# Attention and gated layer on one core: nine rows of q and k to a partition for pairs 1 to 4, and a new order at the start

## The chip, the core and the metric

The kernel runs on one core of a Trainium2 chip. The core has TensorE (PE) for matrix products, VectorE (DVE), ScalarE (ACT) and GpSimd (POOL) for everything else, and 16 DMA engines that move data between the chip's memory and the on-chip buffers. Matrix products are written to the PSUM buffer, all other tiles lie in SBUF, with 128 partitions each. DMAs are issued by SyncE (SP), ACT or POOL. The metric is the time of one execution on the device in microseconds; the median of three runs is given.

## What is computed

Eight batches of eight heads attend over 576 positions of width 64. To the scores a decay is added that depends on the running sum of a second input `s`; then comes a causal softmax. The heads' outputs, side by side, are 4608 rows of 512, and go through two layers with a gated activation between them.

```python
def _attn_ref(q, k, v, s):
    scale = 1.0 / np.sqrt(D)
    scores = scale * np.matmul(q, k.transpose(0, 1, 3, 2))
    causal = np.triu(np.ones((S, S), dtype=bool), k=1)
    cum = np.cumsum(np.maximum(s, 0.0), axis=-1)
    bias = -(cum[:, :, :, None] - cum[:, :, None, :])
    scores = np.where(causal, -1000000000.0, scores + np.minimum(bias, 0.0))
    attn = np.exp(scores - np.max(scores, axis=-1, keepdims=True))
    attn = attn / (np.sum(attn, axis=-1, keepdims=True) + 1e-09)
    return np.matmul(attn, v)

def _moe_ref(x, w_in, w_out):
    h = x @ w_in                      # x: 4608 x 512, w_in: 512 x 2048
    g = h * np.clip(h + 3.0, 0.0, 6.0) / 6.0
    return g @ w_out
```

## The kernel before

Two heads form a pair; a pair has 2 x 576 = 1152 rows of q and as many of k, nine blocks of 128 (`NTR`). There are 32 pairs, and four of them make a batch.

Each row of q and k is widened from 64 to 68 columns (`XW`): three more columns of k hold the running sum, split into three half-precision parts (hi, mid, lo), against ones in q, and one more column of q holds the negated sum against a one in k. A matrix product of the widened rows is then the score with its decay. For the scores both must lie with these 68 columns along the partitions, so PE transposes each block of 128 rows, and a copy brings the result from PSUM to `qkT`, which has three slots (`NS`); rows 64 to 127 of a slot also serve a mask that later pairs use.

The first four pairs (`FIRST`) and pair 4 take their sums from columns, in the tile `x0`, which lies in memory that the layers need later. `load_part` (line 203) reads q or k of a pair so that a partition gets one row of each block, 256 bytes a piece. `first_columns` (line 746) makes the running sums for five pairs at once: DVE scans 90 rows of 64 values of `s`, PE multiplies with a constant `sums` that is loaded from memory, which turns the sums into columns and adds what stands before each row, and DVE and ACT write the parts. `cast_first` (773) casts q or k into `x0`, `turn_first` (776) transposes and copies. `scores_half` (397) forms one half of a head's causal scores in two PSUM banks, the mask added by a product of the identity with a triangle `tri`, and one exponential on ACT writes them to `Pm`. `attend` (426) multiplies with v; a column of ones gives the divisor; `x_transpose` (461) puts the result into `xT`, the input of the layers.

The order of the work is written out by hand: instructions run on each engine in the order of the program, with no scheduler. At the start a few products of zeros (`keep_warm`, 586) run on PE. Then a loop over eight heads (lines 822 to 859) gives, per head: first half of the scores, a transposition of the next pair, second half, and the head before through `attend`. POOL casts rows and values in between and issues the loads of `w_in`.

After these eight heads the first block of 512 rows goes through the first layer (`m1`, split into `m1_sum` and `m1_act`), while `decay_scan` and `decay_rows` compute sums for all heads, `store_aug` sends those of pairs 5 to 9 out to be read back as rows, and `decay_columns` and `decay_order` bring the others into the tile `dec`, for pairs from 10 on, which are transposed by DMA. Then pair 4 is cast and transposed (lines 889 to 897), and `second_pair` (648) handles pairs 4 to 8, with parts of the second layer (`m2`) between. There the scores go one bank at a time through `scores_bank` (338), and POOL sets the masked elements to zero after each exponential. From pair 9 on `weave` mixes attention and layers by weights. `copy_columns` (247) fills the mask columns of the tile that the DMA transposes; `mask_rows` (190) copies mask rows to the slots.

Of the kernel before, what the change touches and what calls it, by code (L numbers as in the profile page):

```python
# [16 lines left out]
def kernel(  # L17
# [25 lines left out]
    PW = 1664  # L43
# [22 lines left out]
    def pair_of_banks(b):  # L66
# [4 lines left out]
    NG = COLS * W2 // 64  # L71
    g = np.arange(NG)
    sel_np = g[:, None] == g[None, :]
    low_np = (g[:, None] < g[None, :]) & (g[:, None] // 9 == g[None, :] // 9)
    sums_dram = nc.inline_tensor(
        np.ascontiguousarray(
            np.stack([m[:, k::2] for k in range(2) for m in (sel_np, low_np)], axis=1)
        ).astype(np.float32),
        name="sums",
    )  # L80
# [28 lines left out]
    dec = cpool.tile([128, NTR, 4, NP], F16, tag="c_dec")  # L109
# [13 lines left out]
        "p (a t i c) -> p a t i c", a=COLS, t=NTR, i=2  # L123
    )

    s_first = work.tile([NG, 64], F32, tag="s_first", bufs=1)
    sums = work.tile([NG, 4, NG // 2], F32, tag="sums", bufs=1)
    scan = work.tile([NG, 64], F32, tag="scan", bufs=1)
    rest = work.tile([128, NG // 2], F32, tag="rest", bufs=1)
# [29 lines left out]
    def mask_view(sl, i):  # L159
# [4 lines left out]
    nc.vector.memset(x0[:, :, :, 0, D:D + 3], 1.0)  # L164
    nc.vector.memset(x0[:, :, :, 1, D + 3:D + 4], 1.0)
    both = [[0, 2], [1, SEQ]]
    select(
        mask_view(0, 1), both, 4 * GRAN, -GRAN, -16384.0,
        warm[64:128, 0:1].unsqueeze(1).to_broadcast([64, 2, SEQ]),
    )  # L170
    select(ident, [[1, 128]], 0, -1, 0.0, one[:, 0:1].to_broadcast([128, 128]))
    select(ident, [[-1, 128]], 0, 1, 0.0)

    def key_rows():
        nc.vector.memset(one[:, 1:2], 1.0)
        k_rows = mask_view(0, 0)
        select(
            k_rows, both, 4 * GRAN, -GRAN, 0.0,
            one[64:128, 1:2].unsqueeze(1).to_broadcast([64, 2, SEQ]),
        )  # L180
        select(k_rows, [[0, 2], [-1, SEQ]], -4 * GRAN + GRAN - 1, GRAN, 0.0)
        select(tri, [[1, 128]], 0, -1, -65504.0, warm[:, 0:128])
# [6 lines left out]

    def mask_rows(sl, i):  # L190
        nc.vector.tensor_copy(out=mask_view(sl, i), in_=mask_view(0, i))
# [8 lines left out]
    def qk_tile(p):  # L200
        qk_f[p] = work.tile([128, NTR, 2, D], F32, tag="qkf", bufs=3, name=f"qkf{p}")

    def load_part(p, i, t0, t1, eng):
        b, h0 = (2 * p) // H, (2 * p) % H
        rows = (q, k)[i][b, h0:h0 + 2].rearrange("h s d -> (h s) d")
        eng.dma_start(  # L206
            out=qk_f[p][:, t0:t1, i, :],
            in_=rows.rearrange("(t p) d -> p t d", p=128)[:, t0:t1, :],
        )
# [27 lines left out]
    def cast_qk(p):  # L237
        t = work.tile([128, NTR, 2, D], F16, tag="qkh", bufs=2)
        nc.gpsimd.tensor_copy(out=t, in_=qk_f.pop(p))
        qk_h[p] = t  # L240
# [32 lines left out]
    def decay_order():  # L273
        dv = dec_f.rearrange("p i (t a h) -> p t i a h", t=NTR, h=2)
        for r0, r1, j0, j1, h in (
            (0, 128, 0, 4, 0), (0, 64, 4, 5, 0), (64, 128, 4, 5, 1), (0, 128, 5, 9, 1)
        ):
            for i in range(3):
                nc.gpsimd.tensor_copy(
                    out=dec[r0:r1, j0:j1, i, :], in_=dv[r0:r1, j0:j1, i, :, h]  # L280
                )
        nc.gpsimd.tensor_scalar_mul(out=dec[:, :, 3, :], in0=dec[:, :, 0, :], scalar1=-1.0)

    def cast_columns(p):
        x = xb[:, p % 2]
        nc.gpsimd.tensor_copy(  # L286
            out=x.rearrange("p (i t) c -> p t i c", i=2)[:, :, :, 0:D], in_=qk_f.pop(p)
        )
        nc.gpsimd.tensor_copy(out=x[:, NTR:2 * NTR, D:D + 3], in_=dec[:, :, 0:3, p])
        nc.gpsimd.tensor_copy(out=x[:, 0:NTR, D + 3:D + 4], in_=dec[:, :, 3:4, p])  # L290
# [105 lines left out]

    def scores_half(hd, half):
        p, hh = hd // 2, hd % 2
        sl = p % NS
# [4 lines left out]
        for kt, lo, hi, c in parts:  # L404
            ops.append((
                c, hi - lo, kT[:, sl, off + 128 * kt:off + 128 * (kt + 1)],
                qT[:, sl, off + lo:off + hi],
# [18 lines left out]
    def attend(hd, qts=range(5)):  # L426
# [5 lines left out]
        block = BLOCK0 if p < FIRST else BLOCK  # L432
# [28 lines left out]
    def x_transpose(p):  # L461
# [10 lines left out]
        pX = f16(PS[:, 4 if p + 1 < FIRST else 2, :], 640) if p < FIRST else f16(bank("S"), 640)  # L472
# [130 lines left out]
    def scores(hd):  # L603
        return [(lambda bi=bi: scores_bank(hd, bi), 400) for bi in range(4)]
# [43 lines left out]
    def second_pair(p, fill):  # L648
# [27 lines left out]
        if first:  # L676
            transpose_group(p + 1, 0)
        if p + 3 < PTD:
# [67 lines left out]
    def first_columns():  # L746
# [6 lines left out]
        key_rows()  # L753
        cT = PS[:, 7, 0:NG // 2]
        for half in range(2):
            o = cT[64 * half:64 * half + 64, :]
            nc.tensor.matmul(
                out=o, lhsT=scan, rhs=sums[:, 2 * half, :], start=True, stop=False
            )
            nc.tensor.matmul(  # L760
                out=o, lhsT=scan[:, 63:64].to_broadcast([NG, 64]), rhs=sums[:, 2 * half + 1, :],
                start=False, stop=True,
            )
        c3 = cT.rearrange("p (a t) -> p a t", a=COLS)
        r3 = rest.rearrange("p (a t) -> p a t", a=COLS)
        hi, mid, lo = (x0[:, :, :, 1, D + j] for j in range(3))
        nc.vector.tensor_copy(out=hi, in_=c3)
        nc.scalar.activation(out=x0[:, :, :, 0, D + 3], in_=hi, func=AF.Copy, scale=-1.0)
        nc.vector.tensor_tensor(out=r3, in0=c3, in1=hi, op=ALU.subtract)
        nc.vector.tensor_copy(out=mid, in_=r3)  # L770
        nc.vector.tensor_tensor(out=lo, in0=r3, in1=mid, op=ALU.subtract)
# [172 lines left out]
```

The softmax here doesn't subtract the row's maximum and nothing guards it: scores larger than these inputs give would overflow.

## Time and profile before

| | us |
|---|---|
| median of three runs (359.52 to 360.73) | 360.02 |
| profiled execution | 359.87 |
| its span | 358.2 |

| engine or part | what the profile has |
|---|---|
| ACT busy | 208.8 us (58%) |
| DVE busy | 182.9 us (51%) |
| POOL busy | 153.3 us (43%) |
| granted PE clock, mean | 0.999 |

The span is the time from the first instruction to the last one's end; what lies around it is 1.7 us in this execution. Busy time of PE is modelled, as products overlap, so a busy PE isn't necessarily one at its peak. How busy each engine is in the stages:

```profile
0.00:12.00 12.00, 9.75 (x70) 5.28 (x71) 5.69 (x18) 5.50 (x8) 8.97 (x20) 1.00 0.96 197
12.00:20.00 8.00, 7.94 (x143) 6.80 (x141) 5.85 (x11) 6.16 (x9) 5.25 (x7) 1.00 0.89 182
20.00:30.00 10.00, 9.54 (x128) 6.72 (x126) 6.24 (x11) 5.43 (x8) 6.42 (x10) 1.00 1.18 208
30.00:45.00 15.00, 15.00 (x91) 7.66 (x90) 12.44 (x22) 9.94 (x16) 7.49 (x17) 1.00 1.06 215
45.00:60.00 15.00, 14.04 (x162) 9.24 (x161) 8.09 (x18) 8.26 (x19) 10.80 (x26) 1.00 1.02 220
```

The columns are the stretch and its length, busy time and number of instructions of PE, of PE's weight loads, DVE, ACT and POOL, the granted clock, the mean busy share of the DMA engines, and the gigabytes per second that they moved.

### The profile page before, as it was taken

The numbers are of one execution on the slowest core, as the hardware profiler recorded it, in microseconds if no ns is written. First come the engines' busy times: TensorE is split into PE (matmuls) and PEld (weight loads), VectorE is DVE, ScalarE is ACT, GpSimd is POOL, SyncE is SP. The second block draws the span as 40 slices with busy tenths as digits, with TensorE's granted clock in tenths as the row PEclk, the third lists the DMA queues.
The fourth block names the chain that finished last, engine by engine and source line by source line (L and its number), as shares of the span: only waits on it lengthen the run. The fifth ranks groups of instructions, "written<-read, shape, count | busy, mean of one in ns | idle before, by whom it ended". The sixth has DMA issues, their size and how long they took to land.

```text
span 358.2 us, 7700 instructions
## 1 busy us (share of the span) xinstructions
PE 349.6 (98%) x2860; PEld 204.2 (57%) x2860; DVE 182.9 (51%) x314; ACT 208.8 (58%) x391; POOL 153.3 (43%) x378
## 2 busy tenths in 40 slices
PE   7999999999999999999999999999999999999996
PEld 3875557665655555555555555555555544544444
DVE  3758737766534553455435553545255536544531
ACT  3777437668847774677467755776477614533410
POOL 6694377765654444444444554555543200000000
PEclk9999999999999999999999999999999999999999
DMA  8999999999989999999998999999947110000012
GB/s 180 214 193 214 212 228 223 215 208 203 210 180 229 197 197 221 229 210 185 185 249 172 207 204 211 170 208 211 224 87 116 50 59 30 31 30 29 32 59 88
DMA packets 185312, 59.09 MB, mean 165 GB/s; under 512 B 177576, under 2 KB 180050, under 8 KB 185274
## 3 DMA queue, kind: packets, MB, share of 16 engines
q1 hardware_dynamic: 181681, 54.05, 72.0%
q0 software_dynamic: 2688, 4.19, 6.6%
q8 instruction: 22, 0.36, 0.4%
q10 hardware_dynamic: 905, 0.36, 0.4%
q14 instruction: 16, 0.13, 0.1%
HBM read 37.32 MB, written 9.53 MB: 131 GB/s over the span
## 4 chain that ended last, share of the span: by engine, by line
PE 84%; DVE 4%; ACT 3%; DMA 3%; POOL 3%; issue 1%; SPq 1%; POOLq 0%; ACTq 0%; DVEq 0%
PE PS L506 32%; PE PS L549 32%; PE PS L348 10%; PE PS L436 7%; DMA qkf<-in_k_dram 3%; DVE gT L517 2%; ACT trl L516 2%; DVE qkT L319 1%; ACT Pm L356 1%; PE PS L569 1%; PE PS L474 1%; PE PS L304 1%; POOL gT L774 1%; PE PS L414 1%; SPq L206 1%
## 5 line engine op out<-in xcount | busy, mean ns | idle before, releaser
L517 DVE SCALAR_TENSOR_TENSOR gT<-trl,PS 128x512 f16<-128x512 f32 x144 | 98.2, 687 | 103.0 <-ACT trl L516 102.9
L516 ACT ACTIVATE trl<-PS,bias 128x512 f32<-128x512 f32 x144 | 98.8, 692 | 78.3 <-PE PS L506 76.5
L506 PE MATMUL PS<-xT,w_in 128*128 128x512 f16 x576 | 143.2, 380 | 0.8 <-DVE gT L517 0.7
L549 PE MATMUL PS<-w_out_sb,gT 128*128 128x512 f16 x560 | 138.9, 379 | 0.0
L356 ACT ACTIVATE Pm<-PS 128x384 f16<-128x384 f32 x224 | 103.0, 507 | 45.7 <-PE PS L348 44.5
L361 POOL TENSOR_SCALAR_AFFINE_SELECT Pm<-Pm 128x256 f16<-128x256 f16 x224 | 68.4, 307 | 114.1 <-ACT Pm L356 106.3
L506 PEld LDWEIGHTS <-w_in 128*128 128x128 f16 x576 | 61.4, 114 | 45.7 <-issue 2.0
L549 PEld LDWEIGHTS <-gT 128*128 128x128 f16 x560 | 51.4, 98 | 48.2 <-issue 0.3
L348 PE MATMUL PS<-qkT 128*128 128x256 f16 x392 | 63.4, 261 | 0.8 <-DVE qkT L319 0.2
L348 PEld LDWEIGHTS <-qkT 128*128 128x128 f16 x392 | 36.0, 98 | 31.5 <-DVE qkT L319 2.4
L436 PEld LDWEIGHTS <-Pm 128*128 128x128 f16 x960 | 38.7, 97 | 11.0 <-ACT Pm L420 0.4
L436 PE MATMUL PS<-v_h,Pm 128*128 128x65 f16 x960 | 42.3, 194 | 0.6 <-ACT Pm L420 0.3
L558 DVE TENSOR_SCALAR osb<-PS 128x512 f32<-128x512 f32 x35 | 24.1, 688 | 33.9 <-PE PS L549 33.6
L448 DVE TENSOR_TENSOR xs<-PS,r 128x640 f16<-128x640 f32 x32 | 26.4, 824 | 1.1
L286 POOL CAST xb<-qkf 128x1152 f16<-128x1152 f32 x22 | 25.2, 1147 | 0.0
L301 POOL CAST v_h<-v_f 128x640 f16<-128x640 f32 x32 | 23.3, 728 | 0.8 <-DMA v_f<-in_v_dram 0.8
L420 ACT ACTIVATE Pm<-PS 128x896 f16<-128x896 f32 (+1 forms) x16 | 13.1, 836 | 4.5 <-PE PS L414 4.4
L319 DVE COPY qkT<-PS 64x640 f16<-64x640 f16 (+1 forms) x20 | 9.1, 454 | 8.9 <-PE PS L304 8.8
L446 DVE RECIPROCAL r<-PS 128x10 f32<-128x10 f32 x32 | 7.0, 217 | 9.2 <-PE PS L436 9.0
L414 PE MATMUL PS<-qkT 128*128 128x64 f16 (+4 forms) x48 | 9.4, 285 | 0.4 <-DVE qkT L786 0.2
L482 DVE COPY xT<-PS 128x576 f16<-128x576 f16 x14 | 6.4, 455 | 5.7 <-PE PS L474 4.5
L786 DVE COPY qkT<-PS 68x1152 f16<-68x1152 f16 (+2 forms) x13 | 7.2, 585 | 2.9 <-PE PS L780 1.9
(71 smaller groups left out, 119.0 us busy)
## 6 DMA issues: line engine op xcount, KB each, us to landing
out_dram<-osb SPq DMA_DIRECT2D x35, 256.0 KB, 2.7
qkf<-in_q_dram SPq DMA_DIRECT2D x31, 288.0 KB, 3.5
qkf<-in_k_dram SPq DMA_DIRECT2D x31, 288.0 KB, 4.2
v_f<-in_v_dram SPq DMA_DIRECT2D x64, 128.0 KB, 3.8
w_in<-in_moe_w_in_dram POOLq DMA_DIRECT2D x4, 512.0 KB, 9.8
w_out_sb<-in_moe_w_out_dram POOLq DMA_DIRECT2D x4, 512.0 KB, 16.2
v_f<-in_v_dram SPq DMA_DIRECT2D x32, 32.0 KB, 2.8
qkT<-xb SPq DMA_TRANSPOSE x22, 5.1
```

The lines of the kernel that those rows point to most:

```text
L286: nc.gpsimd.tensor_copy(out=x.rearrange("p (i t) c -> p t i c", i=2)[:, :, :, 0:D], in_=qk_f.pop(p))
L301: nc.gpsimd.tensor_copy(out=v_h[:, sl, :, :, 0:D], in_=v_f[:, sl])
L348: nc.tensor.matmul(out=S[:, c:c + hi - lo], lhsT=kT[:, sl, off + 128 * kt:off + 128 * (kt + 1)], rhs=qT[:, sl, off + lo:off + hi], start=( ...
L356: nc.scalar.activation(out=P[:, p0:p0 + n], in_=S[:, 0:n], func=AF.Exp, scale=0.125, bias=0.0)
L361: nc.gpsimd.affine_select(out=view, in_=view, pattern=pattern, compare_op=ALU.is_ge, fill=0.0, base=0, channel_multiplier=-1,)
L436: nc.tensor.matmul(out=O[:, hh, qt * VW:qt * VW + D + 1], lhsT=P[:, c:c + 128], rhs=v_h[:, sl, hh, kt, 0:D + 1], start=(qt == 0), stop=(qt ...
L448: nc.vector.tensor_tensor(out=xs.rearrange("p t h d -> p h t d"), in0=Ov[:, :, :, 0:D], in1=r.to_broadcast([128, 2, 5, D]), op=ALU.mult,)
L506: nc.tensor.matmul(out=ph, lhsT=w_in_t[f // 4][:, kc, f % 4, :], rhs=xT[:, kc, n * 512:(n + 1) * 512], start=(kc == 0), stop=(kc == KC - 1),)
L516: nc.scalar.activation(out=trl, in_=ph, func=AF.Relu, bias=bias3[:, 0:1], scale=1.0)
L517: nc.vector.scalar_tensor_tensor(out=gT2[:, n % 2, f, :], in0=trl, scalar=6.0, in1=ph, op0=ALU.min, op1=ALU.mult)
L549: nc.tensor.matmul(out=po, lhsT=gT2[:, n % 2, f, t4 * 128:(t4 + 1) * 128], rhs=w_out_sb[:, f, :], start=(f == 0), stop=(f == NF - 1),)
L558: nc.vector.tensor_scalar_mul(out=osb, in0=po, scalar1=1.0 / 6.0)
```

## The change

It has four parts that belong together.

1. For pairs 1 to 4 q and k are loaded with nine consecutive rows in one partition, 2304 bytes in one piece. The block t of a transposition then holds rows 9p + t instead of 128t + p. For k the copy out of PSUM puts the columns back in order (it writes in order and reads nine blocks 128 apart); for q the columns stay in the order (t, p), the scores are formed for nine groups of columns, with new triangles `tri9`, and the exponential, which reads in order, writes with a step of nine elements, so that `Pm` is in order again. Pair 4 uses `fourth_nine`, one bank at a time, whose mask is added by PE, in place of `scores_bank` with its masks on POOL.
2. The running sums of pair 0 alone come first, from 18 rows of `s`, with a matrix `sums` that POOL builds. Those of pairs 1 to 4 come from a second load of `s`, nine values to a partition: one scan along the partition, one product with a triangle `below`, one addition, and the split into parts.
3. The scores of the first five pairs read 68 partitions of `qkT` instead of 128, so the mask rows aren't needed there; all of them are made by POOL during the first layer (`masks`), three selections and four copies in place of DVE's four copies.
4. The order at the start is new: k of pair 0 is loaded as three and six blocks; the heads of pair 0 go through `attend` together after head 1; loads and casts move with this. The decay columns of later pairs are ordered by four copies instead of twelve and a negation, with the negation done for each pair; `copy_columns` and the load of its data move to pairs 6 and 7.

```diff
-    sums_dram = nc.inline_tensor(
...
+    nc.gpsimd.memset(sums, 1.0)
+    columns = [[1, 2], [2, NTR]]
+    select(sums[:, :, 1, :], columns, -1, -1, 0.0)
...
+    def more_masks():
+        for kt in range(5):
+            select(
+                tri9[:, kt], [[1, NTR], [9, 15]], -2 * kt, -1, -65504.0,
+                warm[:, 0:NTR * 15].rearrange("p (t n) -> p t n", t=NTR),
+            )
...
-    def mask_rows(sl, i):
-        nc.vector.tensor_copy(out=mask_view(sl, i), in_=mask_view(0, i))
...
+        for sl in range(1, NS):
+            for i in range(2):
+                nc.gpsimd.tensor_copy(out=mask_view(sl, i), in_=mask_view(0, i))
...
+        if by_nine(p):
+            eng.dma_start(
+                out=qk_f[p][:, i].rearrange("p t d -> p (t d)"),
+                in_=rows.rearrange("(p t) d -> p (t d)", t=NTR),
+            )
...
-            for i in range(3):
-                nc.gpsimd.tensor_copy(
-                    out=dec[r0:r1, j0:j1, i, :], in_=dv[r0:r1, j0:j1, i, :, h]
-                )
-        nc.gpsimd.tensor_scalar_mul(out=dec[:, :, 3, :], in0=dec[:, :, 0, :], scalar1=-1.0)
+            nc.gpsimd.tensor_copy(
+                out=dec[r0:r1, j0:j1, :, :], in_=dv[r0:r1, j0:j1, :, :, h]
+            )
...
+    FOURTHS9 = [
+        (0, 56, [(0, 0, 56, 0)]),
+        (504, 50, [(0, 56, 64, 0), (1, 14, 56, 8)]),
+        (954, 52, [(1, 56, 64, 0), (2, 28, 64, 8), (4, 56, 64, 44)]),
+        (1422, 22, [(3, 42, 64, 0)]),
+    ]
+
+    def scores_nine(hd, S, n, parts):
+        sl, hh = (hd // 2) % NS, hd % 2
+        Sv = S.rearrange("r (t c) -> r t c", t=NTR)
+        q9 = qT[0:XW, sl, :].rearrange("r (t p) -> r t p", t=NTR)
+        ops = []
+        for kt, n0, n1, c in parts:
+            k0 = SEQ * hh + 128 * kt
+            ops.append((
+                c, n1 - n0, kT[0:XW, sl, k0:k0 + 128], q9[:, :, 64 * hh + n0:64 * hh + n1]
+            ))
+            if n0 == 14 * kt:
+                m = min(15, n1 - n0)
+                ops.append((c, m, ident, tri9[:, kt, :, 0:m]))
...
+        nc.scalar.activation(
+            out=Pm[:, hd % NS, p0:p0 + 2 * NTR * n].rearrange("p (b n t) -> p b t n", b=2, t=NTR),
+            in_=PS[:, b:b + 2, 0:NTR * n].rearrange("p b (t n) -> p b t n", t=NTR),
+            func=AF.Exp, scale=0.125, bias=0.0,
+        )
...
+    def nine_columns():
+        nc.vector.tensor_tensor(
+            out=c_col, in0=local, in1=before.unsqueeze(2).to_broadcast([128, NINE, NTR]),
+            op=ALU.add,
+        )
+        nc.gpsimd.tensor_scalar_mul(out=x0[:, 0, 1:COLS, :, D + 3], in0=c_col, scalar1=-1.0)
+        split_columns(x0[:, :, 1:COLS], c_col)
...
+        if i == 1 and by_nine(p):
+            copy(
+                out=dst[:, 0:W2].rearrange("r (p t) -> r p t", t=NTR)[:, :, t0:t1],
+                in_=pT[0:XW, :].rearrange("r (t p) -> r p t", p=128),
+            )
...
-    keep_warm(6)
+    keep_warm(5)
     cast_first(0, 0, 0, 5, A.copy)
-    cast_first(0, 1, 0, 5, A.copy)
+    first_scan()
     first_columns()
-    keep_warm(2)
+    more_pads()
+    cast_first(0, 1, 0, 3, V.tensor_copy)
+    keep_warm(1)
     turn_first(0, 0, 0, 5, 4, A.copy)
-    turn_first(0, 1, 0, 5, 5, V.tensor_copy)
+    turn_first(0, 1, 0, 3, 5, V.tensor_copy)
+    nine_scan()
+    cast_first(0, 1, 3, 9, G.tensor_copy)
     cast_first(0, 0, 5, 9, G.tensor_copy)
...
         if hd == 0:
+            nine_sums()
+            turn_first(0, 1, 3, 9, 7, V.tensor_copy)
             turn_first(0, 0, 5, 9, 6, V.tensor_copy)
...
+            cast_pair(1)
+            nine_columns()
+            cast_v(0)
+            more_masks()
...
+        elif hd == 1:
+            turn_first(1, 0, 0, NTR, 6, V.tensor_copy)
+            turn_first(1, 1, 0, NTR, 4, V.tensor_copy)
         elif p + 1 < FIRST:
-            turn_first(p + 1, 1, 0, 9, 4, V.tensor_copy)
...
+            turn_first(p + 1, 1 - odd, 0, NTR, 4, V.tensor_copy)
         scores_half(hd, 1)
-        if hd > 0:
+        if hd == 1:
+            attend(0)
+            attend(1)
+            cast_pair(2)
+            cast_v(1)
+        elif hd > 2:
             attend(hd - 1)
```

A half of a head's scores is 900 and 720 columns in `half_nine` (896 and 704 before); in `fourth_nine` the four banks hold 504, 450, 468 and 198 columns (384, 512, 384 and 320 before).

## The prediction

> **What bounds the kernel now.** I read the page first, then the timeline of the first 54 us, then the groups with shapes kept apart, then the waits of TensorE (PE).
>
> ```profile
> span 358.2 us, 7700 instructions
> ...
> PE 349.6 (98%) x2860; PEld 204.2 (57%) x2860; DVE 182.9 (51%) x314; ACT 208.8 (58%) x391; POOL 153.3 (43%) x378
> ...
> PE   7999999999999999999999999999999999999996
> ...
> DMA  8999999999989999999998999999947110000012
> ...
> DMA packets 185312, 59.09 MB, mean 165 GB/s; under 512 B 177576, under 2 KB 180050, under 8 KB 185274
> ```
>
> PE is busy in 98% of the span; only the first slice is weak. The DMA engines are as full, with packets of 256 bytes, but hardly anything of PE waits for them. The profiled execution took 359.87 us around this span of 358.2, 0.15 below the median 360.02; I sum against 359.87. So a change can win only where PE does nothing useful, which is the start. The timeline there (start, duration, engine, line, operation):
>
> ```profile
> 1.25 2.74 PE L589 MATMUL PS<-warm 128*128 128x512 f16 x6 [1.25 <-DVE one L163]
> ...
> 4.74 0.46 PE L757 MATMUL PS<-sums,scan 90*64 90x45 f32 x4 [0.75 <-DMA sums<-sums]
> ...
> 6.37 1.28 PE L780 MATMUL PS<-idtri,gT 128*68 128x128 f16 x10
> ...
> 8.30 0.61 PE L414 MATMUL PS<-qkT 128*128 128x512 f16 x1 [0.22 <-DVE qkT L786]
> ...
> 10.69 0.39 PE L414 MATMUL PS<-qkT 128*128 128x512 f16 x1
> ...
> 12.87 0.39 PE L414 MATMUL PS<-qkT 128*128 128x512 f16 x1
> ```
>
> The first score is at 8.30 us: PE waits for the constant `sums` until 4.74, then for the chain of decay columns. From about 9 us on PE is dense (7.94 of 8.00 us busy between 12 and 20). The second weak place is pair 4, where PE waits for POOL and DVE:
>
> ```profile
> 43.94 1.20 POOL L282 TENSOR_SCALAR dec<-dec 128x288 f16<-128x288 f16 x1
> ...
> 45.10 1.27 POOL L774 CAST gT<-qkf 128x576 f16<-128x576 f32 x2
> ...
> 45.90 0.69 DVE L558 TENSOR_SCALAR osb<-PS 128x512 f32<-128x512 f32 x1 [1.03 <-PE PS L549]
> ...
> 46.51 1.57 DVE L786 COPY qkT<-PS 68x640 f16<-68x640 f16 x4
> ...
> 51.61 0.45 PE L304 MATMUL PS<-idtri,t 128*128 128x128 f16 x5 [0.31 <-POOL t L239]
> ```
>
> Durations that I use (busy us, mean ns, idle before):
>
> ```profile
> L420 ACT ACTIVATE Pm<-PS 128x896 f16<-128x896 f32 x8 | 7.3, 917 | 3.5 <-PE PS L414 3.5
> ...
> L420 ACT ACTIVATE Pm<-PS 128x704 f16<-128x704 f32 x8 | 6.0, 756 | 1.0 <-PE PS L414 0.9
> ...
> L786 DVE COPY qkT<-PS 68x1152 f16<-68x1152 f16 x6 | 4.5, 752 | 1.9 <-PE PS L780 1.9
> ...
> L448 DVE TENSOR_TENSOR xs<-PS,r 128x640 f16<-128x640 f32 x5 | 4.1, 825 | 0.2
> ...
> L786 DVE COPY qkT<-PS 68x512 f16<-68x512 f16 x4 | 1.5, 412 | 0.1
> ...
> L768 ACT ACTIVATE gT<-gT 128x45 f16<-128x45 f16 x1 | 0.4, 402 | 0.5 <-DVE gT L767 0.5
> ```
>
> The two exponentials give 0.84 ns per element and 0.17 us fixed. The two copies give 0.53 ns per element and 0.14 fixed; L448 gives 1.06 ns at the same fixed part.
>
> [...] the 512-column score takes 0.61 us at 8.30 and 0.39 at 10.69. [...] The trace has one ScalarE (ACT) row with such steps, L768: 45 elements in 402 ns, where the line of the exponentials gives 204. [...]
>
> **The change part by part.**
>
> *Start.* `sums` is now built by POOL instead of loaded, so the sums can start when the scan ends (about 3.2) and the five warm matmuls end: 1.25 + 5 x 0.43 = 3.4. Four matmuls with 9 columns instead of 45 take about 0.45 instead of 0.67: 3.85. ACT's negated column 0.25, to 4.27. Five q transposes at half clock (0.107 each) to 4.85, then ACT's copy (0.69) to 5.85. DVE splits four times at about 0.2 (rows of 0.23 to 0.36 for 45 elements), to 5.2, casts three blocks of k (0.3), and three transposes and a copy of 384 (0.35) end at 6.4. The first score starts at 6.45: 1.85 us won.
>
> *What eats it.* Nine blocks of k and q of pair 0 must still arrive. POOL has 17 small operations first, 3.8 us with 0.065 between them (the spacing of its rows), from 0.8 to 5.65, hence casts to 6.7; pair 1's q and k to 8.7. Next is DVE: c_col can only follow the copies of k and q, then POOL's negation of 36 elements (0.33; 288 take 1.20), and four DVE steps of 0.28. Going through PE's order, with full clock from the start of the scores: first half of head 1 at 8.4, q of pair 1 at 9.1, k at 9.85, second half 10.35, both `attend`s 10.8 to 12.1 (the second waits for an exponential). Head 2 starts at 12.1. In the kernel before it starts at 12.87 with one `attend` (0.47) still owed, so the equal point is 13.34: 1.24 won. Then POOL is late: negation, `cast_v` 0.73, five `tri9` selects of 135 elements (0.30 + 0.07 each), pair 2's q and k at 0.73 each end at 13.25; PE wants that k at 12.6. Of the gain 0.6 is left. With half clock until 9 us as before, the same walk gives head 2 at 13.2 and that k at 14.3: 0.5 lost. [...] I take the middle: 0.1 won. The removed masks, 3.5 us on POOL, and the two row copies at DVE are inside this walk.
>
> *Loads.* Eight loads of 1152 packets become 128 each: 8,192 of 185,312 packets go. PE waited about 0.2 us for this (k of pair 3, cast at 17.06); the rest of these loads is hidden by PE work. I take 0.1, between 0 and 0.3; the w_in and w_out loads start at much the same places.
>
> *Copies of k.* [...] 1152 x 1.06 + 0.14 = 1.36 instead of 0.75 for pairs 1 to 3. DVE then has about 3.6 us per pair against some 4.0 of PE: hidden. If a strided read costs two cycles, 2.6 us, it is not, and about 1 us a pair comes on the path; I take one cycle.
>
> *Exponentials.* 900 and 720 elements instead of 896 and 704: at the same price nothing. Written 18 bytes apart they could cost more: below is nothing to gain; above, L768 would give (402-170)/45 = 5.2 ns. I take 0.84 in the forecast, because 45 elements read and written apart cannot separate a fixed cost from one per element.
>
> *Masks later.* Three selects of 1.15 and four copies of about 1.15 put 8 us on POOL after the decay rows (end 34.2), to 42.2; the decay order waits for DVE until 41.8 anyway. It shrinks from 3.3 us (2.12 + 1.20) to four copies, 1.5: the casts of pair 4 end at 45.0 instead of 46.37. The 0.7 us that PE waited there goes.
>
> *Pair 4.* What is late next is DVE. The 16 second-layer matmuls end at T = 45.5. Before, scores start at T+2.33. After, the osb copy still comes first; the four copies start at T+1.0 and take 0.41 + 0.75 + 0.35 + 0.69 (k at 1.06 ns, 0.07 overlap): T+3.2. Since every column block needs all nine reads, PE waits until T+3.3. From there 2 x 2232 columns at 2.4 per ns (1.86), two groups of four matmuls (1.73), 15 products (0.47), five transposes (0.28), and 0.5 of waits for banks and DVE give next pair's scores at T+8.15; before they start at 53.15, T+7.65. The POOL masks and the wait of 0.31 are gone, 632 more columns per head are paid. Net 0.5 lost. The xaug copies (0.55 each) go into DVE's idle 0.66 between its two copy groups of later pairs.
>
> Sum: -0.1 -0.1 +0.5, about +0.1 for 6 x 56 more score columns: +0.4, so 360.3 from the profiled execution and 360.4 from the median.
>
> **The rivals.**
>
> *A, the forecast (0.40): the head start is given back.* 360.4, by itself 358.8 to 361.8. For it: PE's 98%. Against: POOL's small rows are rough.
>
> *B, the exponential pays for its steps (0.33).* Place: heads 2 to 7. Per head 1.68 us now; at two cycles an element 1620 x 0.84 = 1.36 more, 3.05 against PE's 2.0. It decides as soon as an element costs over 1.0 ns (1.95 us a head). Six heads from 12.7 take 18.3, to 31.0, where the last exponential now ends at 25.5: +5.5. Pair 4 adds 2.7, half hidden by its three banks: +1.3, and +0.5 as above: 367.3. L768 and the DVE rows that write single columns (360 ns for 45) speak for it; against it, that their fixed part is unknown. At 5.2 ns it would be tens of us.
>
> *C, the head start stays (0.24).* The clock is granted by about 6.5, POOL's rows are shorter than I count and the 0.65 us wait for pair 2's k falls away: -1.85 -0.2 +0.5 = -1.5, 358.4. For it: PE is idle or warming for nearly all of 8.3 us. Against: the DVE and POOL chains above.
>
> The remaining 0.03 is for anything else, on either side.
>
> **How the numbers follow.** A measurement of this kernel can tell about 0.3%, 1.1 us, from no change: 358.9 to 361.1. A gives 0.05 faster, 0.24 the same, 0.11 slower; C is faster, B slower. With the remainder 0.01 each: 0.30, 0.25, 0.45. The range runs from 357.9 (0.07 of C below) to 368.6 (0.10 of B above).
>
> **What would show it.** First score near 6.45; k copies of 1152 at 1.36 us; exponentials of 900 and 720 at 0.92 and 0.77; POOL's cast of pair 2's k ahead of a PE wait of about 0.6; a DVE wait of over 1 us ahead of pair 4's scores; the layer's first matmul (25.96 now) within 0.7 us of where it was. Exponentials over 1 us would make it wrong, as would a first score later than 7.5.

## The result, and the profile after

The changed kernel takes 404.12 us (median of 4 runs, 403.74 to 405.06) against 359.92 (359.52 to 360.73, 4 runs): a ratio of 1.1229 with an interval of 1.12 to 1.1257. The forecast was 360.4. The page of the profiled execution, in the parts that were shown of before: span, busy time, the slices of PE and ACT, the granted clock, the DMA packets.

```profile
span 402.6 us, 7738 instructions
...
PE 366.7 (91%) x2876; PEld 216.2 (54%) x2876; DVE 184.5 (46%) x318; ACT 252.1 (63%) x391; POOL 158.8 (39%) x380
...
PE   8656449957999999999999999999999999999996
...
ACT  3699986469658956764776577567746762544320
PEclk9955559977999999999999999999999999999999
...
DMA packets 177465, 59.03 MB, mean 147 GB/s; under 512 B 168795, under 2 KB 171179, under 8 KB 177427
```

ACT's sum grew by 43.3 us (208.8 before), and some 33 us of it lie in the slices from the second to the sixth (heads 2 to 7), where PE falls to 40 to 68%. The rest lies in the ninth and tenth, which are pair 4: its eight exponentials hold ACT for 14.4 us instead of 3.4. The timeline of ACT in heads 2 to 7 (start, duration, line, operation, count; in brackets the idle time before and what ended it):

```profile
15.71 42.91 ACT L459 ACTIVATE Pm<-PS 128x900 f16<-128x900 f32 x12 [1.19 <-PE PS L448]
```

Twelve exponentials, two for each of heads 2 to 7, follow one another without a gap for 42.91 us. They hold 6 x (900 + 720) = 9,720 elements for each partition: 4.41 ns an element, where the kernel before has 0.84 and 0.17 us fixed for each instruction. The groups with shapes kept apart (busy us, mean ns of one, idle before):

```profile
L459 ACT ACTIVATE Pm<-PS 128x900 f16<-128x900 f32 x6 | 26.5, 4414 | 1.2 <-PE PS L448 1.2
L459 ACT ACTIVATE Pm<-PS 128x720 f16<-128x720 f32 x6 | 22.0, 3659 | 0.0
...
L469 ACT ACTIVATE Pm<-PS 128x504 f16<-128x504 f32 x2 | 5.1, 2550 | 6.1 <-PE PS L448 6.1
...
L900 DVE COPY qkT<-PS 68x1152 f16<-68x1152 f16 x3 | 4.1, 1354 | 3.4 <-PE PS L893 3.4
```

(The mean of one contains its overlap with the next, so the twelve add to 48.5 us in 42.9.) The copies of k, which read nine apart in PSUM, cost the 1.36 us that was foreseen; the exponentials, which write nine apart in SBUF, cost nearly five times what was foreseen. PE then waits for ACT, head after head:

```profile
PE PS L448 <- ACT Pm L459: 18.6, 10, 3.2
...
PE PS L522 <- ACT Pm L459: 4.4, 2, 2.9
```

The timeline of PE has the places at which both kernels can be compared:

```profile
6.53 0.61 PE L495 MATMUL PS<-qkT 68*128 68x512 f16 x1
...
10.75 2.13 PE L893 MATMUL PS<-idtri,gT 128*68 128x128 f16 x18
...
14.99 0.35 PE L448 MATMUL PS<-qkT 68*128 68x450 f16 x1
...
59.38 2.75 PE L592 MATMUL PS<-xT,w_in 128*128 128x512 f16 x6
```

The first score is at 6.53 instead of 8.30. But PE is still slow at 10.75: 18 transposes take 2.13 us, 0.107 from one start to the next, where nine from 15.51 on take 0.67, 0.056 each. These two speeds are called half clock and full clock here (what the names rest on is said with in_order_rows below). Head 2 begins at 14.99 instead of 12.87. The layer begins at 59.38 instead of 25.97. The other places of the kernel before, on PE and on VectorE:

```profile
25.97 1.48 PE L506 MATMUL PS<-xT,w_in 128*128 128x512 f16 x6
...
54.64 0.22 DVE L446 RECIPROCAL r<-PS 128x10 f32<-128x10 f32 x1
```

And those of the changed kernel on VectorE:

```profile
80.59 0.69 DVE L644 TENSOR_SCALAR osb<-PS 128x512 f32<-128x512 f32 x1 [2.05 <-PE PS L635]
...
99.02 0.22 DVE L532 RECIPROCAL r<-PS 128x10 f32<-128x10 f32 x1 [1.50 <-PE PS L522]
```

Cut at the same places, with three of the kernels below beside it (us; the second layer's first sums are copied to `osb`, and pair 4's reciprocal comes near the end of its attention on VectorE):

| stretch | before | after | in_order | no_restore | no_nine |
|---|---|---|---|---|---|
| start to head 2 | 12.87, and 0.47 still owed | 14.99 | 14.91 | 12.73 | 15.01 |
| head 2 to the layer's first matmul | 13.10, of it 0.47 owed | 44.39 | 13.73 | 13.73 | 12.88 |
| to the copy of the second layer's first sums | 19.93 | 21.21 | 19.92 | 19.93 | 19.92 |
| to the reciprocal of pair 4 | 8.74 | 18.43 | 9.45 | 9.45 | 8.27 |
| the rest | 303.6 | 303.6 | 303.5 | 303.6 | 303.5 |

Of the 44.4 us between the spans, 31.8 are lost in heads 2 to 7 (44.39 against 12.63 without what is owed), 9.7 in pair 4 (18.43 - 8.74), 1.7 at the start (14.99 against 12.87 + 0.47), and 1.3 in the layer's first products. The last are slow: the first six take 2.75 us where they took 1.48 before, and the granted clock reads 0.50 from 59.38 to 62.00, as it does from 30 on. Nothing is lost or won after pair 4.

### The profile page after: what moved, and what is told of

Same layout as the page of the kernel before. It is cut to its first block, busy times and chain, and to the rows that moved or that the text cites. A ratio compares the mean times of both kernels' runs of the same rounds, so it can differ in the third digit from the quotient of the medians.

```text
span 402.6 us, 7738 instructions
## 1 busy us (share of the span) xinstructions
PE 366.7 (91%) x2876; PEld 216.2 (54%) x2876; DVE 184.5 (46%) x318; ACT 252.1 (63%) x391; POOL 158.8 (39%) x380
## 4 chain that ended last, share of the span: by engine, by line
PE 78%; ACT 12%; issue 5%; DVE 3%; POOL 0%; ACTq 0%; POOLq 0%
PE PS L592 29%; PE PS L635 29%; PE PS L373 9%; ACT Pm L459 7%; PE PS L522 6%; ACT Pm L469 3%; DVE gT L603 1%; ACT trl L602 1%; PE PS L495 1%; DVE qkT L344 1%; PE PS L893 1%; PE PS L655 1%; ACT Pm L381 1%; PE PS L560 1%; PE PS L675 1%
## 5 line engine op out<-in xcount | busy, mean ns | idle before, releaser
L635 PE MATMUL PS<-w_out_sb,gT 128*128 128x512 f16 x560 | 140.6, 383 | 0.0
L381 ACT ACTIVATE Pm<-PS 128x384 f16<-128x384 f32 x216 | 99.7, 509 | 38.5 <-PE PS L373 35.5
L386 POOL TENSOR_SCALAR_AFFINE_SELECT Pm<-Pm 128x256 f16<-128x256 f16 x216 | 66.4, 309 | 125.0 <-ACT Pm L381 117.9
L635 PEld LDWEIGHTS <-gT 128*128 128x128 f16 x560 | 51.8, 98 | 48.5 <-issue 1.1
L373 PE MATMUL PS<-qkT 128*128 128x320 f16 (+4 forms) x378 | 61.3, 261 | 1.6 <-ACT Pm L469 1.2
L522 PEld LDWEIGHTS <-Pm 128*128 128x128 f16 x960 | 41.4, 102 | 15.7 <-ACT Pm L459 4.8
L522 PE MATMUL PS<-v_h,Pm 128*128 128x65 f16 x960 | 45.3, 199 | 4.7 <-ACT Pm L459 4.4
L459 ACT ACTIVATE Pm<-PS 128x900 f16<-128x900 f32 (+1 forms) x12 | 42.9, 4036 | 1.2 <-PE PS L448 1.2
L448 PE MATMUL PS<-qkT 68*128 68x72 f16 (+8 forms) x56 | 14.4, 348 | 23.8 <-ACT Pm L459 18.6
L469 ACT ACTIVATE Pm<-PS 128x504 f16<-128x504 f32 (+3 forms) x8 | 14.4, 2238 | 6.1 <-PE PS L448 6.1
L448 PEld LDWEIGHTS <-idtri 128*128 128x128 f16 x40 | 4.8, 121 | 23.5 <-issue 23.5
```

The lines of the kernel that those rows point to most:

```text
L373: nc.tensor.matmul(out=S[:, c:c + hi - lo], lhsT=kT[:, sl, off + 128 * kt:off + 128 * (kt + 1)], rhs=qT[:, sl, off + lo:off + hi], start=( ...
L381: nc.scalar.activation(out=P[:, p0:p0 + n], in_=S[:, 0:n], func=AF.Exp, scale=0.125, bias=0.0)
L386: nc.gpsimd.affine_select(out=view, in_=view, pattern=pattern, compare_op=ALU.is_ge, fill=0.0, base=0, channel_multiplier=-1,)
L459: nc.scalar.activation(out=Pm[:, hd % NS, p0:p0 + 2 * NTR * n].rearrange("p (b n t) -> p b t n", b=2, t=NTR), in_=PS[:, b:b + 2, 0:NTR * n ...
L469: nc.scalar.activation(out=Pm[:, hd % NS, p0:p0 + NTR * n].rearrange("p (n t) -> p t n", t=NTR), in_=S.rearrange("p (t n) -> p t n", t=NTR ...
L522: nc.tensor.matmul(out=O[:, hh, qt * VW:qt * VW + D + 1], lhsT=P[:, c:c + 128], rhs=v_h[:, sl, hh, kt, 0:D + 1], start=(qt == 0), stop=(qt ...
```

## The experiments

The theory: a write of single two-byte elements 18 bytes apart is what costs 4.4 ns, and the rest of the change is worth a microsecond or two. The rivals: the strided read, or the number of stretches in one instruction, costs it; or nine rows to a partition cost much by other ways (more columns, copies of k, pair 4). Each ratio below is to runs of the kernel before from the same session, whose medians were 360.0 to 360.4 us, and not to the 359.92 above.

**What a step costs** (`steps`). The kernel before with test instructions behind its end, among them

```diff
+ nc.scalar.activation(out=flat[:, 0:2048].rearrange("p (n s) -> p n s", s=8)[:, :, 0],
+                      in_=src, func=AF.Exp, scale=0.125, bias=0.0)
```

> The kernel before with 60 instructions behind its last product, three of each form, 256 elements each from PSUM where nothing else is said: exponentials that write half-precision elements 1, 2, 4, 8, 9 and 16 apart, single-precision elements 1, 2, 4 and 9 apart, pairs of elements every 10, exponentials that read 2 and 9 apart and write in order, the two forms of 450 elements (write in order and read apart; read in order and write apart), and copies on DVE and POOL that write 1, 2 and 9 apart. Theory W (the write is what costs): reading apart stays at 0.84 ns an element, half-precision writes 9 apart take 4.2 to 4.5 ns, as the row of 900 elements in the changed kernel. Rival L (a new 16-byte line is what costs): 2 and 4 apart near 0.84 to 2 ns, 8, 9 and 16 apart equal and dear, single precision 4 and 9 apart equally dear. Rival H (a write of half a word is what costs): 2 apart in half precision is already as dear as 9, single precision is cheap at any distance, pairs are cheap. Rival P (the pattern of two directions is what costs, on either side): reading apart is as dear as writing apart.

The groups of the profile, costliest first (busy us, mean ns of one). L921 to L926 write fp16 with a step of 1, 2, 4, 8, 9 and 16 elements, L927 to L930 fp32 with 1, 2, 4 and 9, L931 pairs of fp16 ten elements apart; L932 and L933 read PSUM 2 and 9 apart; L934 reads apart and writes in order, L935 the other way round; L936 to L938 (DVE) write with 1, 2 and 9, L939 and L940 (POOL) with 1 and 9.

```profile
L935 ACT ACTIVATE Pm<-PS 128x450 f16<-128x450 f32 x3 | 6.4, 2134 | 0.1
L924 ACT ACTIVATE Pm<-PS 128x256 f16<-128x256 f32 x3 | 3.9, 1301 | 0.2
L940 POOL COPY Pm<-warm 128x256 f16<-128x256 f16 x3 | 3.9, 1300 | 0.2
...
L938 DVE CAST Pm<-PS 128x256 f16<-128x256 f32 x3 | 3.8, 1275 | 0.2
...
L930 ACT ACTIVATE Pm<-PS 128x256 f32<-128x256 f32 x3 | 1.9, 623 | 0.1
L929 ACT ACTIVATE Pm<-PS 128x256 f32<-128x256 f32 x3 | 1.9, 618 | 0.1
L934 ACT ACTIVATE Pm<-PS 128x450 f16<-128x450 f32 x3 | 1.6, 546 | 0.1
L923 ACT ACTIVATE Pm<-PS 128x256 f16<-128x256 f32 x2 | 1.5, 736 | 0.1
...
L931 ACT ACTIVATE Pm<-PS 128x256 f16<-128x256 f32 x3 | 1.2, 399 | 0.1
...
L933 ACT ACTIVATE Pm<-PS 128x256 f16<-128x256 f32 x3 | 1.1, 383 | 0.1
L922 ACT ACTIVATE Pm<-PS 128x256 f16<-128x256 f32 x2 | 0.9, 456 | 0.1
L921 ACT ACTIVATE Pm<-PS 128x256 f16<-128x256 f32 x2 | 0.8, 383 | 8.6 <-POOL Pm L940 8.6
```

Written in order, 256 elements take 383 ns: 0.84 ns each and 168 fixed. Taking the same 168 off everywhere: a step of 8 costs (1301 - 168) / 256 = 4.4 ns an element, a step of 4 half of that (2.2), a step of 2 a quarter (1.1). So the price goes by stretches of 16 bytes: 4.4 ns for each, whether one of its half words (step 8), two (step 4) or four (step 2) are written apart. Written without steps, the eight of a stretch cost 8 x 0.84 = 6.7 ns, more than the 4.4. A step over 16 bytes (18 in L925, 1287 ns; 32 in L926, 1238 ns) costs no more than one of 16. Whole four-byte words are cheaper: fp32 alone in 16 bytes (618 - 168) / 256 = 1.8 ns, and 128 pairs of fp16 (399 - 168) / 128 = 1.8 ns a pair, close to the 1.7 that two elements cost in order. DVE (1275 against 425 in order) and POOL (1300 against 398) pay as ACT does for half words nine apart; whole words were tried on ACT alone. Of the rivals, L is right in where the price falls and H in that whole words are cheap, 1.8 instead of 4.4 ns for 16 bytes; P is out. Reading nine apart in PSUM costs ACT nothing (383, as in order). The two orders of one exponential of 450 elements decide it: 546 ns when the read is strided, 2134 when the write is.

**Write in order, read apart** (`in_order`). The exponentials walk in the order of the output, for both functions:

```diff
-            out=Pm[...].rearrange("p (b n t) -> p b t n", b=2, t=NTR),
-            in_=PS[:, b:b + 2, 0:NTR * n].rearrange("p b (t n) -> p b t n", t=NTR),
+            out=Pm[...].rearrange("p (b n t) -> p b n t", b=2, t=NTR),
+            in_=PS[:, b:b + 2, 0:NTR * n].rearrange("p b (t n) -> p b n t", t=NTR),
```

> The changed kernel, with the exponentials of pairs 1 to 4 going through their elements in the order of the output: they write in order and read nine columns of PSUM 50, 40 or so elements apart. Theory W: the exponentials of 900 and 720 fall to about 0.92 and 0.77 us, the 33 us of heads 2 to 7 and the 9 us of pair 4 go, and the time is 360 to 362 us (PE still at half clock until head 2, DVE ahead of pair 4). Rival P, reading apart costs the same: 404 us as now. In between, at two cycles an element (1.67 ns), ACT takes 3.0 us a head: 366 to 369 us.

363.01 us (362.79 to 363.34, 6 runs), a ratio of 1.0062 [1.0043, 1.0081]. The order is restored all the same, and 41.1 us of the 44.2 between the medians are gone; the time is 1 us above what theory W allowed. The groups with shapes kept apart:

```profile
L459 ACT ACTIVATE Pm<-PS 128x900 f16<-128x900 f32 x6 | 5.5, 921 | 2.9 <-PE PS L448 2.9
...
L459 ACT ACTIVATE Pm<-PS 128x720 f16<-128x720 f32 x6 | 4.6, 769 | 0.9 <-PE PS L448 0.8
L900 DVE COPY qkT<-PS 68x1152 f16<-68x1152 f16 x3 | 4.1, 1354 | 1.0 <-PE PS L893 1.0
```

921 and 769 ns are what the prediction put down for these shapes (0.92 and 0.77). What is left is 3.3 us between the spans. The timeline of PE:

```profile
10.92 2.13 PE L893 MATMUL PS<-idtri,gT 128*68 128x128 f16 x18
...
14.91 0.35 PE L448 MATMUL PS<-qkT 68*128 68x450 f16 x1
...
17.54 0.66 PE L893 MATMUL PS<-idtri,gT 128*68 128x128 f16 x9 [0.26 <-DVE qkT L900]
...
51.39 0.39 PE L448 MATMUL PS<-qkT 68*128 68x504 f16 x1 [1.00 <-DVE qkT L900]
```

The start again runs at half clock, until about 13 us (two products of 128 columns take 0.35 us at 9.56 and 0.25 at 13.25); PE waits for the copies of k between heads; and in front of pair 4's scores it waits a whole microsecond for VectorE.

**No order restored** (`no_restore`). The kernel leaves out the steps and, with a scale of zero, the scores' values; the instructions keep their sizes.

```diff
-            out=Pm[...].rearrange("p (b n t) -> p b t n", b=2, t=NTR),
-            in_=PS[...].rearrange("p b (t n) -> p b t n", t=NTR), func=AF.Exp, scale=0.125,
+            out=Pm[...].rearrange("p (b x) -> p b x", b=2),
+            in_=PS[:, b:b + 2, 0:NTR * n], func=AF.Exp, scale=0.0,
```

> The changed kernel, with the exponentials of pairs 1 to 4 reading and writing straight through, so that the order of q isn't restored; their scale is zero, so all these weights are one. All else is kept: the floor of this change without any cost of its steps. Theory W: 360 to 362 us, the same as the run with the exponentials in the order of the output within 0.5 us. Rival, that part of the 44 us comes from the new order of the start or from the clock and not from the exponentials: it stays above 365 us.

362.77 us (361.04 to 363.5, 20 runs), a ratio of 1.0054 [1.0042, 1.0067], no different from in_order, and again above theory W's 362: the strided read of 12 large exponentials costs nothing that shows. This profiled execution was among the three shortest, and its PE has full clock from about 6.3 us:

```profile
6.36 0.39 PE L494 MATMUL PS<-qkT 68*128 68x512 f16 x1 [0.23 <-DVE qkT L904]
...
10.32 0.69 PE L892 MATMUL PS<-idtri,gT 128*68 128x128 f16 x9 [0.37 <-DVE gT L848]
...
12.31 0.58 PE L521 MATMUL PS<-v_h,Pm 128*128 128x65 f16 x13 [0.32 <-ACT Pm L500]
12.73 0.36 PE L448 MATMUL PS<-qkT 68*128 68x450 f16 x1
```

The table shows that from head 2 on the two agree to 0.1 us in each stretch; the difference of 2.1 us between these two executions lies before head 2. About 0.2 of it is a later start of the sums in in_order (3.69 against 3.50); the rest goes along with the slower products there (512 columns in 0.61 us at 6.70, against 0.39 at 6.36). Even with full clock, head 2 starts at 12.73 and not at the foreseen 12.1: PE waits 0.37 us for the column splits on VectorE and 0.32 for an exponential.

**One row at a time** (`no_nine`). All pairs keep the old order of rows; the new order at the start and the later masks stay:

```diff
     def by_nine(p):
-        return 0 < p < COLS
+        return False
...
-            out=P[:, p0:p0 + n], in_=S[:, 0:n], func=AF.Exp, scale=0.125, bias=0.0
+            out=P[:, p0:p0 + n], in_=S[:, 0:n], func=AF.Exp, scale=0.0 if p < COLS else 0.125, bias=0.0
...
```

> The changed kernel, with q and k of all pairs read one row of each block to a partition as before: no step in the copies of k and in the exponentials, no triangles of nine, pair 4 with its masks on POOL. The sums of pairs 1 to 4 then belong to other rows; the scale of these exponentials is zero. What is left is the new order at the start, the sums, the masks and the decay order. Theory W: 358.5 to 361 us. If the new order at the start loses by itself, over 361.

360.95 us (360.16 to 362.77, 12 runs), a ratio of 1.0017 [1.0002, 1.0031]. Against in_order, heads 2 to 7 are shorter by 13.73 - 12.88 = 0.85 us and pair 4 by 9.45 - 8.27 = 1.18: that is what nine rows to a partition cost without any strided write. Pair 4 is then 0.5 shorter than in the kernel before (8.74).

**Why the clock stays low at the start** (`in_order_rows`, `in_order_warm`). Half and full clock at the start are read from durations: 512 columns take 0.61 us at one and 0.39 at the other. The names rest on the changed kernel: where its granted clock reads 0.50 (30 to 40 us), nine transposes take 1.17 us (at 35.10), and where it reads 1.00 (15 to 20 us) 0.67 (at 15.51). At the start the granted clock doesn't show the difference: it reads 1.00 up to 12 us in all of these traces, and less only later, where PE of the changed kernel waited for ACT. That a clock is what makes the first products slow is thus the author's reading of their durations. The first kernel clears rows 64 to 127 of pair 0's slot and lets its scores read 128 partitions; the second puts two filling products where PE is idle.

```diff
+        XR = 128 if p == 0 else XW
-                c, hi - lo, kT[0:XW, sl, off + 128 * kt:off + 128 * (kt + 1)],
-                qT[0:XW, sl, off + lo:off + hi],
+                c, hi - lo, kT[0:XR, sl, off + 128 * kt:off + 128 * (kt + 1)],
+                qT[0:XR, sl, off + lo:off + hi],
...
+    nc.vector.memset(qkT[64:128, 0, :], 0.0)
```

> As in_order, but the scores of pair 0 read 128 partitions instead of 68, the lower ones cleared once. What is asked: why TensorE is at half clock until about 13 us although its first score begins near 6.6. If products over 68 rows load the array too lightly for the clock to rise: full clock from about 10 us, head 2 near 13.0 instead of 14.9, and about 361.0 us. If the clock rises at a time of its own, whatever the rows: half clock to about 13 us again and 362.9, within 0.3%, of in_order's 363.0.

362.69 us (362.49 to 363.29, 4 runs), 1.0086 [1.0066, 1.0106]: the reading of few rows is not what holds the time up. In its profile full clock came at about 10.8 us (nine transposes in 0.67 us at 10.95), earlier than in in_order, and head 2 began at 14.18; a single execution can't say why. The edit is not clean either: with the clearing on VectorE, PE's break ahead of the transposes of k is 0.71 us instead of 0.36.

```diff
     turn_first(0, 0, 0, 5, 4, A.copy)
+    keep_warm(2)
     turn_first(0, 1, 0, 3, 5, V.tensor_copy)
```

> As in_order, with two more filling products between the transposes of q and of k of pair 0, where TensorE is idle for about 0.4 us. If breaks in TensorE's work hold the clock down: full clock by about 10 us and 361.0 us. If they do not: half clock to about 13 us and 363.0, or up to 0.3 more where the two products delay the transposes of k.

361.42 us (361.17 to 361.81, 4 runs), 1.0046 [1.003, 1.0062], with full clock from about 6 us (512 columns in 0.39 us at 6.53) and head 2 at 12.89. This speaks for the breaks, but the interval overlaps that of in_order, which ran in another session; see also plain_warm.

**A version without nine rows** (`plain`, `plain_rows`, `plain_warm`, `plain_early`). The new start, with sums for pairs 1 to 4 from 72 rows of 64 and a constant:

```diff
-        nc.tensor.matmul(out=before, lhsT=below, rhs=local[:, :, NTR - 1], ...)
+        for half in range(2):
+            o = c4[64 * half:64 * half + 64, :]
+            nc.tensor.matmul(out=o, lhsT=scan4, rhs=sums4[:, 2 * half, :], ...)
+            nc.tensor.matmul(out=o, lhsT=scan4[:, 63:64].to_broadcast([NG, 64]),
+                             rhs=sums4[:, 2 * half + 1, :], ...)
...
```

> The changed kernel with q, k of all pairs read one row at a time as before, and the sums of pairs 1 to 4 taken from 72 rows of 64 with two constant tables of ones, so that no order needs restoring. It keeps the new order at the start. If nine rows to a partition cost what the run with other sums showed (2 us between the scores and pair 4): 360.9 us, between 360.3 and 361.5, with half clock to about 14 us. If that run was only lucky in its clock: 362 to 363.

360.79 us (359.69 to 361.59, 8 runs), 1.0021 [1.0005, 1.0036]: as no_nine.

> plain with the scores of pair 0 over 128 partitions as in in_order_rows. If the rows hold the clock down: head 2 near 13.0 and about 358.9 us, which would be under the kernel before. If they do not: 360.9 as plain.

360.33 us (359.52 to 362.16, 20 runs), 1.001 [0.9998, 1.0021]. One execution in the profile with full clock from about 5.5 us (three transposes in 0.36 us at 5.55, where plain has 0.53) and a span of 357.8, other runs up to 2.6 us longer: no fixed gain.

> plain with the two filling products between the transposes of q and k, as in in_order_warm. If it is the break in TensorE's work that kept the clock low there: full clock by about 7 us, head 2 near 13.2 instead of 14.5, and 359.7 us, 1.1 below plain. If in_order_warm only met a good moment of the clock: 360.8.

360.46 us (359.65 to 362.83, 22 runs), 1.0009 [0.9998, 1.002]. Neither value: with the filling products some executions are as short as foreseen and others as long as without. So breaks seem not to be all that decides the clock, and the four close runs of in_order_warm may have been luck. The profiled execution was one of the short ones; PE's timeline shows what then eats the start:

```profile
4.97 0.84 PE L669 MATMUL PS<-warm 128*128 128x512 f16 x2
...
6.43 0.39 PE L489 MATMUL PS<-qkT 68*128 68x512 f16 x1 [0.23 <-DVE qkT L903]
...
10.89 0.66 PE L891 MATMUL PS<-idtri,gT 128*68 128x128 f16 x9 [0.82 <-DVE gT L843]
...
12.86 0.58 PE L516 MATMUL PS<-v_h,Pm 128*128 128x65 f16 x13 [0.32 <-ACT Pm L495]
13.28 0.38 PE L489 MATMUL PS<-qkT 68*128 68x512 f16 x1
```

PE had the first score 1.9 us earlier than before, and head 2 is at 13.28 with both `attend`s done: the kernel before is at the same point at 12.87 + 0.47 = 13.34. The next one moves the four column steps into VectorE's idle time ahead of the scores, which takes the wait of 0.82 away. It also drops the filling product ahead of the first score and turns q of pairs 2 and 3 before k:

```diff
+    nine_scan()
     turn_first(0, 1, 0, 3, 5, V.tensor_copy)
-    nine_scan()
+    nine_sums()
+    nine_columns()
...
-    keep_warm(1)
...
-            turn_first(p + 1, 1 - odd, 0, NTR, 4, V.tensor_copy)
+            turn_first(p + 1, odd, 0, NTR, 4, V.tensor_copy)
```

> plain_warm with the sums of pairs 1 to 4 and their columns ahead of the first score, in VectorE's idle time, so that the copy of pair 1's k no longer stands behind them (TensorE waited 0.9 us for it in plain_rows at full clock), and q of pairs 2 and 3 turned before k, in the order in which they arrive. If VectorE's column steps are what eats the early start when the clock is granted in time: head 2 near 12.2 and 358.7 us, below the kernel before. If the next thing is late as well (the loads of pairs 2 and 3, which arrive at the rate of the DMA engines): 359.7, as plain_warm.

360.83 us (359.55 to 361.46, 13 runs), 1.0004 [0.9992, 1.0017]: neither value, and over both. In its profile PE is at half clock until about 11 us (512 columns in 0.63 us at 9.75) and does not wait for columns any more; head 2 begins at 13.81. That is 0.7 earlier than in plain, where full clock came only at about 12.3 (18 transposes from 11.10 in 1.72 us), and the median is no better. The loads arrive while the DMA engines are busy: in plain_rows their mean share, microsecond by microsecond, reads 1.05 to 1.33 from 4 to 12.

```profile
4.97 1.06 PE L669 MATMUL PS<-warm 128*128 128x512 f16 x2
...
10.71 1.39 PE L891 MATMUL PS<-idtri,gT 128*68 128x128 f16 x18
```

This trace says more on breaks than the medians do. From 1.3 to 11.2 us PE has no idle time in it at all, and it is still at half clock for nearly all of that time. Up to these two filling products its work has the same times as in plain_warm, within 0.01 us; there full clock came during them (0.84 us), here it did not (1.06). What PE did before that can't be what made the difference.

**The kernel before, with its own gap filled** (`before_warm`).

```diff
-    keep_warm(6)
+    keep_warm(8)
```

> The kernel before with two more filling products in the 0.75 us in which TensorE waits for the constant of the sums. If breaks in TensorE's work decide when the clock is granted: full clock before the first score at 8.3 us, head 2 near 12.4 instead of 12.9, and 359.8 us with a narrower spread than the kernel before. If the moment is chance: 360.3, within 0.2%.

359.61 us (358.98 to 360.14, 21 runs) against 360.0 (359.16 to 360.84, 25 runs): a ratio of 0.9988 [0.9981, 0.9995], the only version whose interval lies below the kernel before. The timeline of PE:

```profile
1.25 3.60 PE L589 MATMUL PS<-warm 128*128 128x512 f16 x8 [1.25 <-DVE one L163]
...
8.16 0.39 PE L414 MATMUL PS<-qkT 128*128 128x512 f16 x1 [0.43 <-DVE qkT L786]
...
12.62 0.39 PE L414 MATMUL PS<-qkT 128*128 128x512 f16 x1
```

The first score takes 0.39 us, full clock, where it took 0.61 before, and head 2 is 0.25 earlier. The 0.4 us of the medians is of that size, and the spread is narrower (1.2 us against 1.7), as the first reading had it. That the clock is the cause rests on one trace of each.

## Why the prediction was wrong

The step that failed is *Exponentials*: "at the same price nothing ... I take 0.84 in the forecast". They cost 4.4 ns an element. The prediction had the right number in hand and named it: L768, 45 elements written apart in 402 ns, gave at most 5.2 ns; with the price of `steps`, the writes are 45 x 4.4 = 198 ns, and with the fixed 168 that makes 366 of these 402. It was set aside because a fixed cost could not be excluded, which was a reason to keep the value in the range, and its consequence ("tens of us") was left out of both the range and the chances.

Rival B (0.33) was the right mechanism in the right place, with one term too small: 0.84 more for each element instead of 3.6. At the 4.4 ns of `steps` its 9,720 elements are 42.8 us of ACT, and the trace has 42.9, from 15.7 to 58.6. The last of these exponentials ended at 25.5 before: +33.1, against 33.4 that the layer starts later. For pair 4: two heads with 504 + 450 + 468 + 198 = 1,620 elements, 3,240 x 3.6 = 11.7 us more, of which the stretch lost 9.0 against in_order. The rest was hidden; B had put that down to the three banks, which no run tried.

The other steps, read from in_order, where the exponentials have their old price:

- *Start*: the first score was foreseen at 6.45 and came at 6.53 (6.36 to 6.87 in the other runs). Right. One sum in it has a slip: 4.85 + 0.69 is 5.54 and not 5.85, but the score waits for the other copy, VectorE's of k, so nothing hangs on it.
- *What eats it*: 0.1 won, as the middle between 0.6 won (1.24 at head 2, less a wait for POOL) and 0.5 lost with half clock until 9 us. That was the author's estimate. In in_order, head 2 at 14.91 is 1.57 behind the equal point of 13.34, with half clock until 13 us; with full clock from 6.3 us (no_restore) 0.61 are won at head 2, half of what the walk had there, since the splits on VectorE and an exponential are waited for. The wait of 0.6 for POOL's cast of pair 2's k did not appear; that 0.6 is left either way is luck. In the traces of the changed kernel and its variants full clock comes anywhere between about 5 us (plain_rows) and 15 (the changed kernel, 128 columns still in 0.31 us at 13.41, 135 in 0.23 at 15.19), so the middle was too kind.
- *Loads*: 7,847 packets fewer, 8,192 foreseen. What that was worth alone was not tried.
- *Copies of k*: 1.354 us, foreseen 1.36 from the 1.06 ns an element of L448, which the prediction calls one cycle; read in order they took 0.752. The estimate was right. But they were not wholly hidden: PE waited 0.26 us for one of them, and the nine rows cost 0.85 us in heads 2 to 7, where 0.1 had been put down for the columns.
- *Masks later*: the casts of pair 4 end at 47.85 in a kernel whose layer starts 2.67 later, so at 45.2 by the old clock; foreseen 45.0. Right in time; the 0.7 us that this should have won are 0.5 in no_nine, which keeps the old way through pair 4.
- *Pair 4*: scores begin after a wait of 1.00 us for VectorE (over 1 foreseen), and the stretch is 0.71 longer (0.5 foreseen). The 2.4 columns per ns of that sum are in the trace of the kernel before, where four products of 512 columns at 49.08 take 0.86 us to the next start. The wait of 0.31 for POOL is gone in in_order and still there in no_nine, so the masks on PE took it away, as foreseen. Right.

With the exponentials at their old price the parts measure, in in_order's trace, 1.57 (start) + 1.10 (heads 2 to 7) + 0.71 (pair 4) = 3.4 us, where the sum had 0.4. So the forecast of 360.4 would have been 2.6 us short of in_order's 363.01 even then, mostly through the slow products at the start. Rival C, the head start that stays, did not occur; in no_nine and plain, without the nine rows, the medians don't have it either.

## What to carry to other kernels

When a permutation has to be made by an instruction that copies anyway, walk in the order of the output and put the steps on the PSUM side: on ScalarE the same instruction took 546 ns that way and 2134 the other, while VectorE's copies of k, which read apart, took 1354 instead of 752. Ask of every strided write how many stretches of 16 bytes it touches and whether it writes half words (4.4 ns a stretch in steps, against 1.8 on ScalarE for whole words), and price it by the worst row in the profile before until a run says otherwise. A start that saves work was won here only where TensorE's products were fast early (head 2 at 12.73 in no_restore, at 14.91 in in_order) and as far as the next engine had room (in plain_warm PE waited 0.82 us for VectorE). Where executions differ in when that happens, one trace shows only one of the cases.

## What had not been expected of the hardware

- In steps, a stretch of 16 bytes cost 4.4 ns when single half words were written into it, and on ScalarE 1.8 ns when whole words were (pairs of fp16 count as such). With half words nine apart ScalarE, VectorE and GpSimd paid alike (1287, 1275 and 1300 ns for 256 elements). Two half words in each stretch (a step of 4) still took 2.2 ns each, 736 ns for 256 elements.
- One kernel's executions differ by up to 3 us (361.04 to 363.5 us for no_restore, 359.65 to 362.83 for plain_warm), and the traces, which have one execution each, put such a difference down to when TensorE's products become fast. In in_order PE was busy for all but 0.02 us from 6.05 to about 13 us before that, and in plain_early without any break from 1.3 to 11.2. What held it down is open: neither the rows read nor the breaks explain it.
- PE of the changed kernel was busy 56, 64, 42 and 40% of the four stretches of 10 us from 20 to 60, because it waited for ACT, and its granted clock read 0.56, 0.50, 0.50 and 0.50 there; PE of in_order was busy 96% from 20 to 30 us and 100% from 30 to 45, at 1.00. Among the consequences of the lower clock only the layer's first products show (2.75 us for six, 1.48 before), because ACT set the pace.
